# A fused landmark-attention and FFT-mixing kernel: where the landmark sums stand in VectorE's order, and a later due time for the sum of C's transposed parts

## The chip, the cores and the metric

One Trainium2 chip, one of its cores. The metric is the device time of one execution in microseconds (us). Before the change the median of three runs is 1006.84 us (1006.77 to 1008.21). A core has five engines that run side by side, each with its own instruction stream: TensorE (PE, matmuls), VectorE (DVE), ScalarE (ACT), GpSimd (POOL) and SyncE (SP), which here issues the DMAs. An engine takes its instructions in the order in which they stand in its stream; an instruction that waits for another engine holds up all that stand behind it.

## What is computed

Cut to what matters, for q, k, v of 8 batches, 8 heads, 576 positions, head size 64, and landmarks of 18 positions each (32 a head):

```python
q_lm = q.reshape(B, H, 32, 18, D).mean(axis=3)
k_lm = k.reshape(B, H, 32, 18, D).mean(axis=3)
A, Bm, C = sm(q, k_lm), sm(q_lm, k_lm), sm(q_lm, k)    # softmaxes of scaled products
Z = Bm.T / (norm1(Bm) * norminf(Bm) + 1e-6)
for _ in range(6):
    Z = 2 * Z - Z @ Bm @ Z
x = A @ Z @ C @ v                                      # heads side by side: 8 x 576 x 512
u = x + real(fft(fft(x, axis=1), axis=2))
un = (u - mean(u)) / sqrt(var(u) + 1e-6)
out = u + relu(un @ w_ch1) @ w_ch2                     # 512 -> 2048 -> 512
```

## The kernel before

The work is written as Python generators, each for one strand: `tokens(b)` (sums of landmarks, softmax A), `landmarks(b)` (products with the landmark sums, Bm, C, the six steps of Z, then the combined tables and `mix`), `values(b)` (C times v), `mix(b)` (A and the FFT tables give u; then `norm`), and `mlp()`, which takes u two tiles of 128 rows (a chunk) at a time through both weight matrices. `run()` steps the generators in a planner's time, `self.now`, and thereby writes the program down. PE's instructions keep the order in which they are written, so that attention's matmuls are strewn between those of the MLP. The other engines' instructions are put in an order by a scheduler, as far as no dependency and no added rule says otherwise.

The class `Timed` wraps DVE, ACT and POOL (V, A, G in the code). For each instruction it keeps the planned time of its result in `there` and appends its planned start to the engine's `log`. Its added rule is this: if an input is in the set `slow` (a DMA's result, or POOL's), the instruction is put behind the last one of its engine whose planned start is not after that input's planned arrival. The same can be asked for by setting `late` ahead of an instruction; `late` is back at 0 after each. Every instruction that goes through Timed is recorded under line 138, every matmul under 245, so a profile tells them apart by their tiles.

What matters here, with the names of tiles as the profile writes them:

- `load(b + 1)`, called at the end of landmarks(b), issues the DMAs of k, q and v of the next batch into tiles `big`. So k and q are in memory long before tokens(b + 1) is planned.
- In `tokens(b)`, for each half e of the heads: one sum over k (`lm<-big`, 128x64 out of 128x1152) and two over q (128x32 out of 128x576) on DVE, and one |q| with its sum on ACT (`big<-big` 128x1168, which gives `amax`). `kmax<-lm`, `qsum<-amax` and a few steps on 128x1 (`aq_e`, `aq_r`, `kb`) follow, then the splits of q into two 16-bit parts on ACT and DVE (`big<-big,aq_r`, two of 128x1024 and two of 128x128). For b = 1 the sums are kept in program order.
- `landmarks(b)` starts with PE's `at<-lm` and `at<-big,lm`; DVE makes `Bd`, `cmx`, `bmx`, `bs`, `nrm`, `BTd` of them, and PE takes up `at<-nrm,ones_bd` and `at<-BT,BTd`. Then come `RE` and `E`, and PE's six steps `at<-RE,E`.
- `values(b)` from batch 2 on: C (a tile `mid`) is cut into two 16-bit parts by ACT and POOL, these are transposed by DMA (line 588, `mid<-mid`), and DVE adds the transposed parts (`mid<-mid` 128x640). The tile of the transposed parts, th, is in `slow`, with a planned arrival 4.0 us after the parts.
- `mix(b)`: DVE makes `w<-at,scw,w` and `u<-at,scw,w`. The last 64 rows of two batches share one tile u (`uR` in the code), taken from a pool of 7, whose tiles come free when the DMA to `out_dram` has read them. `norm`: `bn`, `mv`, `ve`, `rt`, `r`, `row` on DVE and POOL, then two DMA transposes a tile to `unT`, which the MLP's first matmuls `h<-unT,w` read.
- `mlp()`: h takes two PSUM banks; ACT and DVE make `h<-h` of each. The second matmuls `acc<-w,h` gather into two PSUM banks, acc0 and acc1, of which there is one set: the next chunk's first acc matmul waits until DVE's `u<-acc,wsc,u` has read the bank. The output DMA follows each u.

Of the kernel before, what the change touches and what calls it, by code (L numbers as in the profile page):

```python
# [158 lines left out]
class Kernel:  # L159
# [82 lines left out]
    def mm(self, out, a, b, start=True, stop=True, share=1.0):  # L242
        self.there[out.name] = self.now
        self.now += share * (1.0e-3 if a.dtype == F32 else 0.42e-3) * math.prod(b.shape[1:])
        self.nc.tensor.matmul(out, a, b, start=start, stop=stop, skip_group_check=True)  # L245

    def tr(self, out, a, ident):
        self.there[out.name] = self.now
        self.now += 0.11
        self.nc.tensor.transpose(out, a, ident)  # L250
# [171 lines left out]
    def tokens(self, b, st):  # L422

        nc, mm, mm3, tr, sm, split = self.nc, self.mm, self.mm3, self.tr, self.sm, self.split
        V, A = self.V, self.A
# [5 lines left out]
        qhs = []  # L431
        for e in range(2):
            kf, qf = loads[e][0][:, 0 : 2 * S], loads[e][1][:, 0:NQ]
            first = V.tensor_reduce(lm[:, 1, e], kf.rearrange("p (m t) -> p m t", t=18), AX.X, ALU.add)
            if b == 1:
                self.tc.keep_in_program_order(first)

            lv = lm[:, 0, e].rearrange("p (x o m) -> p x o m", o=2, m=8)
            qv = qf.rearrange("p (x o t) -> p x o t", o=2, t=2 * SEG)
            for o in range(2):  # L440
                first = V.tensor_reduce(lv[:, :, o], qv[:, :, o, o : o + 144].rearrange("p x (m t) -> p x m t", t=18), AX.X, ALU.add)
                if b == 1:
                    self.tc.keep_in_program_order(first)
            qhs.append(self.big().bitcast(F16))
            A.activation((self.whole[0].bitcast(F16) if b == 0 else qhs[e])[:, 0:NQ], qf, AF.Abs, accum_out=am[:, e : e + 1])
            yield self.till(lm)
# [63 lines left out]
        for u in range(3):  # L510
# [8 lines left out]
            if b >= 2 or u == 2:  # L519
                yield self.till(ae)  # L520
                hl = self.row(2 * w, F16).rearrange("p (y t) -> p y t", y=2)
# [43 lines left out]
    def values(self, b, st, loads, Ces, crs, ci):  # L565

        nc, mm, tr, sm = self.nc, self.mm, self.tr, self.sm
        V, A = self.V, self.A
        R0 = sm.tile([P, 2, 64], F32, name="R0", bufs=1)
        ETs = []  # L570
        for g in range(2):
            yield self.till(Ces[g])
            if b < 2:
                ET = self.mid().rearrange("p (t m) -> p t m", t=5)
                ps = self.psum()
                for t in range(4):
                    tr(ps[:, 128 * t : 128 * t + 128], Ces[g][:, 128 * t : 128 * t + 128], self.ident)
                A.copy(ET[:, 0:4].rearrange("p t m -> p (t m)"), ps)
                ps = self.psum()
                tr(ps[:64, 0:128], Ces[g][:, 512:576], self.ident)  # L580
                A.copy(ET[:64, 4], ps[:64, 0:128])
            else:

                hl, th = (self.mid().bitcast(F16).rearrange("p (y t) -> p y t", y=2) for _ in range(2))
                A.copy(hl[:, 0], Ces[g])
                self.G.tensor_tensor(hl[:, 1], Ces[g], hl[:, 0], ALU.subtract)
                for y in range(2):
                    nc.sync.dma_start_transpose(th[:, y].rearrange("p (t m) -> p t m", m=P), hl[:, y])
                self.there[th.name] = self.there[hl.name] + 4.0
                self.slow.add(th.name)  # L590
                V.tensor_tensor(Ces[g], th[:, 0], th[:, 1], ALU.add)
                ET = Ces[g].rearrange("p (t m) -> p t m", t=5)
            ETs.append(ET)
        for g in range(2):
            yield self.till(ETs[g], loads[0][2], loads[1][2], banks=1)
            vfs = [loads[e][2].rearrange("p (c d) -> p c d", c=5) for e in range(2)]
            ps = self.psum()
            for t in range(5):
                n = P if t < 4 else 64
                for i in range(4):  # L600
                    e, at = divmod(sum(GROUPS, []).index(HEADS[g][i]), 4)
                    v = vfs[e][:n, t, 64 * at : 64 * at + 64]
                    mm(ps[32 * i : 32 * i + 32, 0:64], ETs[g][:n, t, 32 * i : 32 * i + 32], v if at % 2 == i % 2 else v[:, ::-1], t == 0, t == 4)
            V.tensor_scalar(R0[:, g], ps[:, 0:64], crs[g], ci[:, g : g + 1], ALU.mult, ALU.mult)
        st["R0"] = R0
# [480 lines left out]
```

## Time and profile before

| | |
|---|---|
| median of three runs | 1006.84 us (1006.77 to 1008.21) |
| the profiled execution | 1008.58 us |
| its span in the trace | 1006.8 us |
| mean granted clock of PE | 0.976 of full speed |
| PE busy | 959.8 us (95%) |
| DVE busy | 600.5 us (60%) |
| ACT busy | 333.0 us (33%) |
| POOL busy | 102.8 us (10%) |

The durations below come from the profiled execution, whose own time is 1.74 us above the median and 1.8 us above its span. A row of a timeline gives the start in us from the span's start, the duration, engine, line, operation, output and inputs, and in brackets the idle time of the engine ahead of it with what ended it; neighbouring instructions of one kind are one row with their count. A row of the waits gives who waits for whom, the sum in us, how many times, and the longest. In a table of windows, PEclk is the clock granted to PE as a share of full speed.

### The profile page before, as it was taken

The page shows a single profiled execution, that of the slowest core. Times are in us where ns is not written, and L with a number is a line of the kernel's source. Part 1 is how long each engine was busy: PE and PEld are TensorE (multiplying, and loading weights), DVE is VectorE, ACT ScalarE, POOL GpSimd, SP SyncE. Part 2 cuts the span into 40 slices and gives each one's busy share as a digit, 9 for nine tenths or more (in the row PEclk, how much of TensorE's full clock was granted, in tenths as well). Part 3 has the DMA queues.
Part 4 walks back from the last instruction along what each step waited for, and adds up shares of the span by engine and source line. Part 5 has one row for each costly group of instructions (what it writes and reads, how often), then busy time and mean ns, then how long its engine had stood idle before and what let it go on. Part 6 is the DMA issues. An engine that isn't in the chain of part 4 may idle for free.

```text
span 1006.8 us, 20849 instructions
## 1 busy us (share of the span) xinstructions
PE 959.8 (95%) x8698; PEld 666.9 (66%) x8698; DVE 600.5 (60%) x1629; ACT 333.0 (33%) x716; POOL 102.8 (10%) x114
## 2 busy tenths in 40 slices
PE   6869989699999999999999999999999999999998
PEld 4658556467766767667666677676666776666665
DVE  7989876878476836388367736684643935241111
ACT  5668543243224322143224222332322323111110
POOL 0000000003011301032012201120020210010000
PEclk8879989989999999999999999999999999999999
DMA  9854104123302340134211340225020200120000
GB/s 330 290 210 145 62 2 169 22 54 83 136 17 48 63 157 12 32 51 100 100 43 29 45 168 9 55 44 187 1 53 22 53 10 22 22 54 21 1 21 21
DMA packets 97774, 74.66 MB, mean 74 GB/s; under 512 B 68112, under 2 KB 86544, under 8 KB 97552
## 3 DMA queue, kind: packets, MB, share of 16 engines
q1 hardware_dynamic: 97680, 73.34, 25.4%
q8 instruction: 68, 1.11, 0.4%
q14 instruction: 26, 0.21, 0.1%
HBM read 48.02 MB, written 9.44 MB: 57 GB/s over the span
## 4 chain that ended last, share of the span: by engine, by line
PE 86%; DVE 9%; ACT 2%; DMA 2%; issue 1%; POOL 1%; SPq 0%; DVEq 0%; ACTq 0%; POOLq 0%
PE acc L245 36%; PE h L245 36%; PE at L245 13%; DVE w L138 2%; DVE mid L138 1%; DVE u L138 1%; DVE lm L138 1%; DMA big<-k_dram 1%; PE at L250 1%; DVE row L138 0%; ACT w L138 0%; DMA mid<-mid 0%; DMA out_dram<-u 0%; DVE asum L138 0%; DVE bn L138 0%
## 5 line engine op out<-in xcount | busy, mean ns | idle before, releaser
L245 PE MATMUL h<-unT,w 128*128 128x256 f16 x3456 | 411.4, 273 | 6.7 <-DMA unT<-row 5.4
L245 PEld LDWEIGHTS <-w 128*128 128x128 f16 (+1 forms) x3584 | 346.0, 99 | 80.9 <-DMA unT<-row 5.8
L245 PE MATMUL acc<-w,h 128*128 128x512 f16 x1632 | 386.2, 382 | 1.8 <-DVE w L138 1.8
L245 PEld LDWEIGHTS <-h 128*128 128x128 f16 x1632 | 157.8, 99 | 166.6 <-issue 14.2
L138 DVE SCALAR_TENSOR_TENSOR h<-h 128x512 f16<-128x512 f32 x136 | 93.6, 688 | 207.1 <-ACT h L138 206.7
L138 ACT ACTIVATE h<-h 128x512 f16<-128x512 f32 x136 | 81.0, 596 | 319.2 <-PE h L245 313.1
L138 POOL TENSOR_TENSOR r<-ve,mhalf 128x2 f32<-128x2 f32 (+1 forms) x20 | 13.8, 689 | 495.7 <-DVE ve L138 477.0
L138 DVE TENSOR_REDUCE lm<-big 128x32 f32<-128x576 f32 (+1 forms) x48 | 44.4, 938 | 3.3 <-DMA big<-k_dram 3.1
L245 PEld LDWEIGHTS <-big 128*128 128x128 f16 (+1 forms) x864 | 40.5, 104 | 8.5 <-issue 2.1
L138 DVE TENSOR_TENSOR mid<-mid 128x256 f32<-128x256 f32 (+3 forms) x64 | 38.4, 633 | 7.9 <-DMA mid<-mid 6.4
L138 POOL TENSOR_TENSOR mid<-mid 128x640 f16<-128x640 f32 (+1 forms) x24 | 30.6, 1292 | 117.0 <-ACT mid L138 102.5
L245 PEld LDWEIGHTS <-mid 64*128 64x128 f16 (+1 forms) x624 | 29.2, 95 | 17.1 <-issue 10.8
L138 POOL TENSOR_TENSOR row<-row 128x512 f16<-128x512 f32 (+1 forms) x33 | 34.1, 1048 | 50.1 <-ACT row L138 50.1
L138 DVE SCALAR_TENSOR_TENSOR u<-at,scw,w 128x128 f32<-128x128 f32 (+3 forms) x105 | 33.7, 388 | 7.2 <-PE at L245 5.5
L138 ACT CAST row<-row 128x512 f16<-128x512 f32 (+1 forms) x40 | 20.8, 551 | 51.6 <-DVE row L138 44.6
L138 DVE SCALAR_TENSOR_TENSOR w<-at,scw,w 128x262 f32<-128x262 f32 (+1 forms) x42 | 19.1, 486 | 29.7 <-ACT w L138 29.6
L138 DVE SCALAR_TENSOR_TENSOR u<-acc,wsc,u 128x512 f32<-128x512 f32 x36 | 26.9, 749 | 11.8 <-PE acc L245 11.7
L245 PE MATMUL at<-mid,big 128*128 128x262 f16 (+1 forms) x288 | 33.2, 289 | 0.0
L245 PEld LDWEIGHTS at<-RE,E 128*128 128x128 f32 x192 | 26.8, 194 | 8.4 <-issue 2.8
L245 PE MATMUL at<-RE,E 128*128 128x64 f32 (+1 forms) x192 | 28.8, 273 | 3.2 <-DVE E L138 2.5
L138 DVE SCALAR_TENSOR_TENSOR big<-big,aq_r 128x1024 f16<-128x1024 f32 (+1 forms) x32 | 25.8, 840 | 3.5 <-ACT big L138 3.5
L138 DVE TENSOR_TENSOR E<-at,mask 128x256 f32<-128x256 f32 x40 | 16.7, 418 | 18.3 <-PE at L245 18.3
(178 smaller groups left out, 916.8 us busy)
## 6 DMA issues: line engine op xcount, KB each, us to landing
w<-w_dram SPq DMA_DIRECT2D x22, 512.0 KB, 7.0
big<-v_dram SPq DMA_DIRECT2D x16, 640.0 KB, 9.5
big<-q_dram SPq DMA_DIRECT2D x16, 584.0 KB, 6.1
big<-k_dram SPq DMA_DIRECT2D x16, 576.0 KB, 5.2
out_dram<-u SPq DMA_DIRECT2D x36, 256.0 KB, 2.0
big<-w_dram SPq DMA_DIRECT2D x10, 512.0 KB, 6.6
t<-t_dram SPq DMA_DIRECT2D x1, 1048.0 KB, 10.6
unT<-row SPq DMA_TRANSPOSE x64, 2.4
```

The lines of the kernel that those rows point to most:

```text
L138: ins = call(out, *args, **kw)
L245: self.nc.tensor.matmul(out, a, b, start=start, stop=stop, skip_group_check=True)
L250: self.nc.tensor.transpose(out, a, ident)
```

## The change

In `tokens`, ahead of the sum over k, `late` of DVE and ACT is set to the planner's present time; ahead of each of the two sums over q, that of DVE is. So each sum, and ACT's sum of magnitudes, is put behind the last instruction of its engine whose planned start is not after that time. In `values`, the planned arrival of the transposed parts of C is set 2.5 us later. The whole diff:

```diff
@@ -431,6 +431,7 @@
         for e in range(2):
             kf, qf = loads[e][0][:, 0 : 2 * S], loads[e][1][:, 0:NQ]
+            V.late = A.late = self.now
             first = V.tensor_reduce(lm[:, 1, e], kf.rearrange("p (m t) -> p m t", t=18), AX.X, ALU.add)
@@ -438,6 +439,7 @@
             for o in range(2):
+                V.late = self.now
                 first = V.tensor_reduce(lv[:, :, o], qv[:, :, o, o : o + 144].rearrange("p x (m t) -> p x m t", t=18), AX.X, ALU.add)
@@ -586,7 +588,7 @@
-                self.there[th.name] = self.there[hl.name] + 4.0
+                self.there[th.name] = self.there[hl.name] + 6.5
                 self.slow.add(th.name)
                 V.tensor_tensor(Ces[g], th[:, 0], th[:, 1], ALU.add)
```

The engines' instructions are the same in number and kind; their order differs. In batch 0 nothing moves, in batch 1 only ACT's first |q|, which goes behind three more splits of weights. From batch 2 on, the sums move on DVE.

The first place is DVE in the mix of batch 1, around the norm of its first two tiles (`w_74` is a part of the second weight buffer that serves as scratch, `r_2574` and `r_2576` are small tiles of the norm). Before:

```order
L138 BN_STATS bn<-u 128x6 x2
L138 BN_AGGR mv<-bn 128x2
L138 TENSOR_REDUCE lm<-big 128x4x8
L138 BN_AGGR mv<-bn 128x2
L138 SCALAR_TENSOR_TENSOR h<-h 128x512
L138 TENSOR_SCALAR ve<-mv 128x2
L138 TENSOR_REDUCE lm<-big 128x4x8
L138 TENSOR_TENSOR rt<-r_2574 128x2
L138 TENSOR_REDUCE lm<-big 128x64
L138 SCALAR_TENSOR_TENSOR rt<-rt,ve 128x2
L138 TENSOR_REDUCE kmax<-lm 128x1
L138 SCALAR_TENSOR_TENSOR r_2576<-rt,r_2574 128x2
```

And after the change, at the same place:

```order
L138 BN_STATS bn<-u 128x6 x2
L138 BN_AGGR mv<-bn 128x2 x2
L138 TENSOR_SCALAR ve<-mv 128x2
L138 SCALAR_TENSOR_TENSOR h<-h 128x512
L138 TENSOR_TENSOR rt<-r_2574 128x2
L138 SCALAR_TENSOR_TENSOR rt<-rt,ve 128x2
L138 SCALAR_TENSOR_TENSOR r_2576<-rt,r_2574 128x2
L138 TENSOR_SCALAR row<-u,mv,r_2576 128x512 x2
L138 TENSOR_TENSOR row<-row 128x512 x2
```

The sums of batch 2 and its kmax are gone from here, and the norm's steps follow one another.

The second place is DVE ahead of the landmarks of batch 2, where they now stand (`acc_2163` and `acc_2164` are acc0 and acc1 of the chunk that ends, `r_2780` and `r_2782` small tiles of the norm of the last rows). Before:

```order
L138 TENSOR_TENSOR rt<-r_2780 128x1
L138 TENSOR_TENSOR kb<-kmax,aq_e 128x1
L138 SCALAR_TENSOR_TENSOR rt<-rt,ve 128x1
L138 SCALAR_TENSOR_TENSOR r_2782<-rt,r_2780 128x1
L138 TENSOR_SCALAR row<-u,mv,r_2782 128x512
L138 SCALAR_TENSOR_TENSOR big<-big,aq_r 128x1024
L138 SCALAR_TENSOR_TENSOR h<-h 128x512
L138 TENSOR_TENSOR row<-row 128x512
L138 SCALAR_TENSOR_TENSOR u<-acc_2163,wsc,u 128x512
L138 SCALAR_TENSOR_TENSOR u<-acc_2164,wsc,u 128x512
L138 SCALAR_TENSOR_TENSOR big<-big,aq_r 128x128
L138 SCALAR_TENSOR_TENSOR big<-big,aq_r 128x1024
```

And after the change:

```order
L138 TENSOR_REDUCE lm<-big 128x64
L138 SCALAR_TENSOR_TENSOR r_2782<-rt,r_2780 128x1
L138 TENSOR_REDUCE lm<-big 128x4x8
L138 TENSOR_SCALAR row<-u,mv,r_2782 128x512
L138 TENSOR_REDUCE lm<-big 128x4x8
L138 SCALAR_TENSOR_TENSOR u<-acc_2163,wsc,u 128x512
L138 TENSOR_TENSOR row<-row 128x512
L138 SCALAR_TENSOR_TENSOR u<-acc_2164,wsc,u 128x512
L138 SCALAR_TENSOR_TENSOR h<-h 128x512
L138 TENSOR_REDUCE kmax<-lm 128x1
L138 TENSOR_TENSOR qsum<-amax 128x1
L138 TENSOR_SCALAR aq_e<-qsum 128x1
```

Three of the six sums stand just ahead of the first u<-acc here, the other three a little before; the splits of q, which stood on both sides of u<-acc, now follow behind `Bd`.

The third place is DVE in the mix of batch 5, around its last 64 rows, ahead of the landmarks of batch 6. Before, the sums of batch 6 stood further ahead, among the steps for the first four tiles:

```order
L138 TENSOR_SCALAR row<-u,mv,r_8389 128x512 x2
L138 SCALAR_TENSOR_TENSOR h<-h 128x512
L138 SCALAR_TENSOR_TENSOR w_74<-at,scw,w_73 64x262 x2
L138 SCALAR_TENSOR_TENSOR u<-at,scw,w_74 64x256
L138 SCALAR_TENSOR_TENSOR u<-at,scw,w_74 64x128 x2
L138 TENSOR_TENSOR qsum<-amax 128x1
L138 BN_STATS bn<-u 128x6
L138 TENSOR_SCALAR aq_e<-qsum 128x1
L138 BN_AGGR mv<-bn 128x2
```

And after the change:

```order
L138 TENSOR_SCALAR row<-u,mv,r_8389 128x512 x2
L138 SCALAR_TENSOR_TENSOR h<-h 128x512
L138 TENSOR_REDUCE lm<-big 128x64
L138 SCALAR_TENSOR_TENSOR w_74<-at,scw,w_73 64x262 x2
L138 SCALAR_TENSOR_TENSOR u<-at,scw,w_74 64x256
L138 SCALAR_TENSOR_TENSOR u<-at,scw,w_74 64x128 x2
L138 TENSOR_REDUCE lm<-big 128x4x8
L138 BN_STATS bn<-u 128x6
L138 TENSOR_REDUCE lm<-big 128x4x8
L138 BN_AGGR mv<-bn 128x2
```

The first three sums now stand among these steps, the other three and kmax some rows further on, still ahead of `qsum`.

## Prediction

> **What bounds the kernel now.** I read the page's span, engine and chain lines first.
>
> ```profile
> span 1006.8 us, 20849 instructions
> ...
> PE 959.8 (95%) x8698; PEld 666.9 (66%) x8698; DVE 600.5 (60%) x1629; ACT 333.0 (33%) x716; POOL 102.8 (10%) x114
> ...
> PE 86%; DVE 9%; ACT 2%; DMA 2%; issue 1%; POOL 1%; SPq 0%; DVEq 0%; ACTq 0%; POOLq 0%
> ```
>
> TensorE (PE) is busy for 95%, and the change takes no matmul away, so the time can only move where PE stands still. VectorE (DVE), 60% busy, is the engine whose order changes. Next, the waits of PE, summed over the span; these rows, and a wait of 2.4 for w that the timeline below shows, are those that the change can shorten.
>
> ```profile
> PE h L245 <- DMA unT<-row: 5.4, 2, 3.2
> ...
> PE at L245 <- DVE E L138: 2.5, 1, 2.5
> ...
> PE at L245 <- DVE u L138: 1.6, 2, 0.8
> ```
>
> In total 5.4 + 2.4 + 2.5 + 1.6 = 11.9 us can be won; where DVE gets later at any other place, time can only be lost. The waits for unT and w lie in the mix of batch 1, shown here in PE's timeline.
>
> ```profile
> 194.92 0.49 PE L245 MATMUL at<-Wx,mid 64*128 64x128 f16 x11 [2.37 <-DVE w L138]
> 198.59 0.40 PE L245 MATMUL h<-unT,w 128*128 128x256 f16 x1 [3.18 <-DMA unT<-row]
> 201.18 1.04 PE L245 MATMUL h<-unT,w 128*128 128x256 f16 x4 [2.19 <-DMA unT<-row]
> ```
>
> **What is moved.** The page's groups of the sums, of the splits of q that follow them on DVE, and of a step of ScalarE:
>
> ```profile
> L138 ACT ACTIVATE h<-h 128x512 f16<-128x512 f32 x136 | 81.0, 596 | 319.2 <-PE h L245 313.1
> ...
> L138 DVE TENSOR_REDUCE lm<-big 128x32 f32<-128x576 f32 (+1 forms) x48 | 44.4, 938 | 3.3 <-DMA big<-k_dram 3.1
> ...
> L138 DVE SCALAR_TENSOR_TENSOR big<-big,aq_r 128x1024 f16<-128x1024 f32 (+1 forms) x32 | 25.8, 840 | 3.5 <-ACT big L138 3.5
> ```
>
> 44.4 us in 8 batches is 5.6 us for each batch's six sums; the four splits of a batch, two long (1.3) and two short (0.3), are 25.8 / 8 = 3.2. They now stand where k and q have just arrived, in gaps of DVE. By the order that results, held against the times at which DVE's neighbouring rows ran, they come some 14 to 46 us later, just ahead of the chain of landmarks(), which PE needs soon after. No DMA moves on SP and nothing is added on POOL. So the sum has one gain and six places where 5.6 us are pushed into a denser stretch.
>
> **Batch 1's mix, the gain.** DVE's timeline there:
>
> ```profile
> 184.66 1.34 DVE L138 TENSOR_REDUCE lm<-big 128x64 f32<-128x1152 f32 x1
> ...
> 189.01 0.72 DVE L138 TENSOR_REDUCE lm<-big 128x32 f32<-128x576 f32 x1
> ...
> 190.38 0.74 DVE L138 TENSOR_REDUCE lm<-big 128x32 f32<-128x576 f32 x1
> ...
> 191.34 0.16 DVE L138 TENSOR_TENSOR rt<-r 128x2 f32<-128x2 f32 x1 [0.22 <-POOL r L138]
> 191.42 1.34 DVE L138 TENSOR_REDUCE lm<-big 128x64 f32<-128x1152 f32 x1
> ...
> 192.80 0.29 DVE L138 TENSOR_REDUCE kmax<-lm 128x1 f32<-128x128 f32 x1
> ...
> 193.47 0.99 DVE L138 TENSOR_SCALAR row<-u,mv,r 128x512 f32<-128x512 f32 x2
> ```
>
> 1.34 + 0.72 + 0.74 + 1.34 + 0.29 = 4.43 us of sums for batch 2 stand ahead of the row that the transposes to unT wait for. Without them the POOL step that now costs 0.22 shows more of itself, so not all is won: I take the rows 3.4 us earlier. PE's three waits there, 2.37 + 3.18 + 2.19 = 7.74, end 3.4 us earlier: **-3.4**. At the start, ScalarE's first sum of magnitudes of batch 1 moves behind three weight splits, which so run sooner, and PE waits for them there: **-0.4**, an estimate between 0 and 0.6, one step of ScalarE.
>
> **Batch 2's landmarks, the first place that pays.** DVE, then PE:
>
> ```profile
> 217.10 1.40 DVE L138 SCALAR_TENSOR_TENSOR u<-acc,wsc,u 128x512 f32<-128x512 f32 x2
> ...
> 223.89 0.18 DVE L138 TENSOR_TENSOR nrm<-diag,rs 128x64 f32<-128x64 f32 x1
> ...
> 218.19 1.46 PE L245 MATMUL acc<-w,h 128*128 128x512 f16 x6
> ...
> 226.02 0.38 PE L245 MATMUL at<-nrm,ones_bd 128*128 128x128 f32 x2
> ```
>
> u<-acc frees the two PSUM banks that the next chunk's acc matmuls need; the first of the two ends at 217.8, 0.4 us ahead of them. Ahead of it now come 5.6 us of sums, while a split of 1.3 us and the small steps around it (1.2) go behind it and 1.4 us of idle time (waits for ScalarE and POOL shortly before) are used up: it is 1.7 us later, so PE waits 1.3 for the first bank and, since one 0.7 us step now stands between the two u<-acc, 0.5 more for the second. Then nrm: it had 226.02 - 224.07 = 1.95 us to spare, but the split work of 3.3 us that was ahead of it now lies inside its chain: it is late by a further 1.2. Together **+3.0**.
>
> **The mixes of batches 2 and 6, with the sums of batches 3 and 7 in them: two like places.** DVE and PE in the first, then the page's row of the output DMA; the second shows the same wait of 0.8, as the row on u above counts it twice.
>
> ```profile
> 317.57 0.75 DVE L138 SCALAR_TENSOR_TENSOR u<-acc,wsc,u 128x512 f32<-128x512 f32 x1
> ...
> 320.45 0.99 DVE L138 SCALAR_TENSOR_TENSOR u<-at,scw,w 64x256 f32<-64x256 f32 x3 [0.83 <-DMA out_dram<-u]
> ...
> 320.98 1.23 PE L245 MATMUL at<-big,lm 64*32 64x288 f32 x16 [0.79 <-DVE u L138]
> ...
> out_dram<-u SPq DMA_DIRECT2D x36, 256.0 KB, 2.0
> ```
>
> A chain is there already: u<-acc, its output DMA (2.0), then the u that takes the freed buffer, whose reading of PSUM frees banks for PE. Three sums and kmax (3.0 us) now come between h and the splits that precede u<-acc; 1.5 us of splits move behind it. u<-acc comes 1.5 us later, and the chain has no slack, since PE waits for it now: **+1.5** each, **+3.0**.
>
> **The landmarks of batches 4 and 6.** DVE's nrm against PE's use of it, and the idle time of DVE in batch 6 that could take the sums in:
>
> ```profile
> 446.26 0.18 DVE L138 TENSOR_TENSOR nrm<-diag,rs 128x64 f32<-128x64 f32 x1
> ...
> 448.67 0.38 PE L245 MATMUL at<-nrm,ones_bd 128*128 128x128 f32 x2
> ...
> 643.79 0.91 DVE L138 SCALAR_TENSOR_TENSOR w<-at,scw,w 64x262 f32<-64x262 f32 x2 [0.70 <-ACT w L138]
> ...
> 647.50 0.16 DVE L138 TENSOR_TENSOR rt<-r 128x1 f32<-128x1 f32 x1 [0.54 <-POOL r L138]
> ...
> 652.68 0.69 DVE L138 SCALAR_TENSOR_TENSOR h<-h 128x512 f16<-128x512 f32 x1 [0.41 <-ACT h L138]
> ...
> 654.76 0.29 DVE L138 TENSOR_SCALAR Bd<-at 128x32 f32<-128x32 f32 x2 [1.39 <-PE at L245]
> ...
> 657.92 0.18 DVE L138 TENSOR_TENSOR nrm<-diag,rs 128x64 f32<-128x64 f32 x1
> ...
> 660.33 0.39 PE L245 MATMUL at<-nrm,ones_bd 128*128 128x128 f32 x2
> ```
>
> In batch 6, DVE's idle time adds up to 0.70 + 0.54 + 0.41 + 1.39 = 3.0 us. Of 5.9 us (sums and kmax), 2.9 stay; the first split then waits about 1 us for ScalarE, whose sum of magnitudes has moved later too, and one split of 0.3 comes into the chain: nrm is 4.0 to 4.2 later against a slack of 660.33 - 658.10 = 2.2: **+1.8**. In batch 4 the slack is 448.67 - 446.44 = 2.2 as well; two splits (1.6) enter the chain and Bd is 3 later: **+2.3**.
>
> **Batch 5, and the sum of C's parts.** DVE, PE, and the windows table (its clock stands third from the end):
>
> ```profile
> 559.57 0.82 DVE L138 TENSOR_TENSOR mid<-mid 128x640 f32<-128x640 f16 x1 [2.23 <-DMA mid<-mid]
> ...
> 551.64 2.75 PE L245 MATMUL acc<-w,h 128*128 128x512 f16 x12
> ...
> 560.87 0.63 PE L245 MATMUL at<-RE,E 128*128 128x64 f32 x4 [2.46 <-DVE E L138]
> ...
> 561.93 4.45 PE L245 MATMUL acc<-w,h 128*128 128x512 f16 x12
> ...
> 562.00:565.40 3.40, 3.40 (x9) 1.21 (x10) 3.40 (x9) 1.47 (x3) 0.00 (x0) 0.50 0.00 0
> ```
>
> Here E stands behind the second sum of C's parts, which waits for its transposes. The raise from 4.0 to 6.5 should put that sum behind E; in the order that results only the first sum moves, past one reciprocal, and the second still precedes E. So I cost this edit at nothing, between -4.2 (the wait of 2.46 and what follows it, below) and +2.5 (the whole raise shows on the path). What counts is that the landmarks before it are later by the sums: transposes, sum and E come 1.7 later, with no slack: **+1.7**.
>
> After that wait of 2.46, the granted clock is 0.50 for one window of 3.4 us, and twelve matmuls take 4.45 in place of 2.75: such a window costs 1.7. The wait of 0.79 in batch 2's mix is not followed by one. The new or grown waits, of 1.2 to 2.3, lie between these two; I count one window for all of them together, **+1.7**, with none and three (5.1) as ends. The Trainium skill ("TensorE: Matmul & The Clock Gate", section "HAM oscillation — how this bites in real kernels") names gaps of more than some 3.4 us as what throttles TensorE. The row of 2.46 speaks against reading that as a safe limit. By that rule this term would be nothing.
>
> **The sum.** -3.4 - 0.4 + 3.0 + 3.0 + 1.8 + 2.3 + 1.7 = +8.0, with the clock +9.7. The profiled execution took 1008.58 (span 1006.8), so it becomes 1018.3. It lies 1.74 above the median of the three runs before, 1006.84, which gives 1016.5.
>
> **Rivals.**
>
> 1. Faster: the queue absorbs the sums. The 14 to 46 us by which they move hold idle DVE time, 40% of the span, and three of my six places have a slack of about 2 us, so that a backlog that is 2 us shorter than I have it costs nothing there. If the sums slip into such gaps and the backlog has drained by the time that u<-acc, Bd and E are reached, only batch 1's gain is left: -3.8, 1003.0; and with one window of half clock less behind its shorter waits, 1001.3. It decides where less than 2.2 us of the 5.9 are left at Bd and none at u<-acc. For it: DVE is idle for 3.0 us just there in batch 6. Against it: 5.9 us are to fit in these 3.0. Chance 0.20.
> 2. No change: a third of the 11.8 comes, about +4, against -3.8: 1007. It would be so if about two of the six places pay, and the others, each a lateness of 1.2 to 2.3 after about 2 us of slack, come out within it. Against it: three of them (both mixes and batch 5) have no slack at all. Chance 0.12.
> 3. The raised 6.5 frees E in batch 5, -4.2: the sum is +5.5 or less, 1012.3. Against it stands the order. Chance 0.10.
> 4. No new stall trips the clock: all of them are shorter than the 2.46 that did. +8.0, 1014.8. Chance 0.18. The rule of the Trainium skill told above, by its page's figure, gives this case.
> 5. My forecast, 1016.5, with one window, more where two or three trip (up to 1020): 0.40.
>
> A change of 0.2%, 2.0 us, is about what a measurement of this kernel can tell from none. Faster takes rival 1, 0.20; the same takes rival 2, 0.12; slower is the rest, 0.68. The likeliest sign's own range is 1011 to 1020. The range takes in all the slower cases up to three windows and reaches down to rival 1's 1003, so that what it leaves out is the lower part of rival 1 and what lies above 1020, together under 0.2: 1002.5 to 1020.
>
> **What would show it.** In the changed kernel PE's waits for unT in batch 1's mix should sum to about 4.4 in place of 7.7; PE should wait for u ahead of the first acc matmul of a chunk in batch 2 and for nrm in batches 2, 4 and 6 by 1 to 2.5 us each, rows that are not there now; the two waits for u in the mixes should be 2.3 in place of 0.8; the wait for E in batch 5 should grow, or be gone (rival 3). If PE shows no wait for nrm, the forecast's sign is wrong. If batch 1's waits stay at 7.7, the gain was not there, and the time is 3.4 higher.

## Result and profile after

The changed kernel takes 1020.37 us (median of 4 runs, 1017.26 to 1022.66), the kernel before beside it 1007.4 us (4 runs, 1006.77 to 1008.21): ratio 1.0126, 95% interval 1.0098 to 1.0155. It is slower, as forecast; the time lies 0.4 us above the upper end of the range and 3.9 above the forecast. The profiled execution took 1017.26 us, the shortest of the four. Its page:

```profile
span 1015.3 us, 20860 instructions
...
PE 961.4 (95%) x8698; PEld 666.9 (66%) x8698; DVE 603.5 (59%) x1629; ACT 331.3 (33%) x716; POOL 100.4 (10%) x114
...
PE 72%; DVE 15%; issue 6%; ACT 3%; POOL 2%; DMA 1%; SPq 0%; DVEq 0%; POOLq 0%; ACTq 0%
```

The work is the same; the span is 8.5 us longer, and in the chain that ended last PE's share falls from 86% to 72% and DVE's rises from 9% to 15%. PE's waits, the rows that moved:

```profile
PE at L245 <- ACT mid L138: 11.3, 5, 4.0
PE at L245 <- DVE u L138: 5.1, 2, 2.6
...
PE h L245 <- DMA unT<-row: 3.6, 2, 2.3
...
PE acc L245 <- DVE u L138: 2.9, 2, 1.5
...
PE at L245 <- DVE E L138: 2.3, 1, 2.3
...
PE at L245 <- DVE w L138: 0.9, 1, 0.9
...
PE at L245 <- DVE nrm L138: 0.4, 1, 0.4
```

Two of these rows before the change, which the prediction doesn't show:

```profile
PE at L245 <- ACT mid L138: 6.2, 2, 4.0
...
PE acc L245 <- DVE u L138: 1.4, 1, 1.4
```

The waits for unT and w fell from 7.7 in all to 4.5; those for u in the mixes rose from 1.6 to 5.1, those for u ahead of acc from 1.4 to 2.9, and those for `mid` of ScalarE from 6.2 to 11.3. The last was not in the prediction's list. Where each lies, in PE's timeline: batch 1's mix and batch 2.

```profile
193.65 0.49 PE L245 MATMUL at<-Wx,mid 64*128 64x128 f16 x11 [0.90 <-DVE w L138]
195.38 0.28 PE L245 MATMUL h<-unT,w 128*128 128x256 f16 x1 [1.25 <-DMA unT<-row]
197.97 3.30 PE L245 MATMUL h<-unT,w 128*128 128x256 f16 x17 [2.31 <-DMA unT<-row]
...
215.22 1.02 PE L245 MATMUL acc<-w,h 128*128 128x512 f16 x4 [1.52 <-DVE u L138]
```

Behind batch 1's shorter waits there is less half clock as well. The windows table gives a stretch, its length, the busy time of PE (then of the other engines), and third from the end the granted clock. Before, the clock was 0.50 for three windows, from 196.8 on; the last two of them, and then the one in the same place after the change, where only the window from 197.2 to 200.6 was at half clock:

```profile
200.20:203.60 3.40, 2.42 (x12) 1.75 (x13) 1.88 (x7) 0.00 (x0) 0.69 (x1) 0.50 0.11 22
203.60:207.00 3.40, 3.40 (x31) 2.18 (x29) 0.00 (x0) 0.47 (x1) 0.00 (x0) 0.50 0.00 0
```

```profile
200.61:204.02 3.41, 3.41 (x41) 2.32 (x40) 1.31 (x3) 1.84 (x4) 0.00 (x0) 1.00 0.00 0
```

And the later places, each with its wait (the mix of batch 2, the landmarks of batches 4, 5 and 6, the wait for E in batch 5, the mix of batch 6):

```profile
321.09 1.23 PE L245 MATMUL at<-big,lm 64*32 64x288 f32 x16 [2.55 <-DVE u L138]
...
449.36 0.16 PE L245 MATMUL at<-kb,ones 128*128 128x1 bf16 x1 [1.65 <-ACT mid L138]
...
451.00 0.46 PE L245 MATMUL at<-nrm,ones_bd 128*128 128x128 f32 x2 [0.16 <-ACT RE L138]
...
553.53 0.16 PE L245 MATMUL at<-kb,ones 128*128 128x1 bf16 x1 [0.91 <-ACT mid L138]
...
564.53 0.63 PE L245 MATMUL at<-RE,E 128*128 128x64 f32 x4 [2.30 <-DVE E L138]
...
665.12 0.16 PE L245 MATMUL at<-kb,ones 128*128 128x1 bf16 x1 [2.10 <-ACT mid L138]
...
789.13 1.23 PE L245 MATMUL at<-big,lm 64*32 64x288 f32 x16 [2.55 <-DVE u L138]
```

The same matmuls read against the rows of before give PE's lag at each place: -3.2 at the last wait for unT (201.18, now 197.97), +0.1 at the mix of batch 2 (320.98, now 321.09), +2.3 at batch 4's nrm (448.67, now 451.00), +3.7 at E (560.87, now 564.53), and +8.5 at the end. So the gain came, was given back by the mix of batch 2, and the rest of the batches added the loss.

In batches 4 to 6 the new wait stands at the small matmul on kb, and its releaser is not kb. Batch 4, DVE's timeline first:

```profile
439.67 2.66 DVE L138 TENSOR_REDUCE lm<-big 128x64 f32<-128x1152 f32 x3
...
443.08 0.14 DVE L138 TENSOR_TENSOR kb<-kmax,aq_e 128x1 bf16<-128x1 f32 x1
444.45 1.28 DVE L138 SCALAR_TENSOR_TENSOR big<-big,aq_r 128x1024 f16<-128x1024 f32 x1 [1.23 <-ACT big L138]
...
446.26 0.28 DVE L138 TENSOR_SCALAR Bd<-at 128x32 f32<-128x32 f32 x2
...
449.13 1.28 DVE L138 SCALAR_TENSOR_TENSOR big<-big,aq_r 128x1024 f16<-128x1024 f32 x1
...
450.67 0.19 DVE L138 TENSOR_TENSOR nrm<-diag,rs 128x64 f32<-128x64 f32 x1
```

Then ScalarE's:

```profile
448.72 0.50 ACT L138 ACTIVATE mid<-at,cb 128x288 f32<-128x288 f32 x1 [0.90 <-DVE cb L138]
```

kb itself was ready at 443.2. But its matmul needs a free PSUM bank. Attention's products share four banks in the kernel, and the four tiles of landmark products fill them until ScalarE's exp of C (`mid<-at,cb`) has read the first; that exp waits for cb, which stands in DVE's late chain. The exp ends at 449.2, and PE goes on at 449.36. Bd is 3.2 us later than before (443.10), nrm 4.4 later (446.26); since PE has already stood 1.65 at kb, only 0.16 is left to wait ahead of nrm.

### The profile page after: what moved, and what is told of

Same layout as the page of the kernel before. It is cut to its first block, busy times and chain, and to the rows that moved or that the text cites. A ratio compares the mean times of both kernels' runs of the same rounds, so it can differ in the third digit from the quotient of the medians.

```text
span 1015.3 us, 20860 instructions
## 1 busy us (share of the span) xinstructions
PE 961.4 (95%) x8698; PEld 666.9 (66%) x8698; DVE 603.5 (59%) x1629; ACT 331.3 (33%) x716; POOL 100.4 (10%) x114
## 4 chain that ended last, share of the span: by engine, by line
PE 72%; DVE 15%; issue 6%; ACT 3%; POOL 2%; DMA 1%; SPq 0%; DVEq 0%; POOLq 0%; ACTq 0%
PE h L245 30%; PE acc L245 30%; PE at L245 12%; DVE w L138 3%; DVE lm L138 2%; DVE u L138 2%; DVE mid L138 2%; DVE big L138 1%; DVE row L138 1%; DVE h L138 1%; POOL row L138 1%; ACT big L138 1%; DVE cmx L138 1%; DMA big<-k_dram 1%; DVE asum L138 1%
## 5 line engine op out<-in xcount | busy, mean ns | idle before, releaser
L138 ACT ACTIVATE big<-big,aq_r 128x1024 f16<-128x1024 f32 (+1 forms) x32 | 23.0, 774 | 17.5 <-DVE kb L138 15.7
```

The lines of the kernel that those rows point to most:

```text
L138: ins = call(out, *args, **kw)
```

## Experiments

Theory: DVE's queue ahead of u<-acc and of the landmarks' chain, lengthened by 5.6 us of sums in each batch from 3 on, makes the loss; batch 2 is even; the due time does nothing; how many of the new waits are followed by a window of half clock sets the rest. Rivals: the later due time has a part, or the late values of the sums, or ScalarE's delayed sums of magnitudes.

**Parts of the change.** Four kernels: the late lines alone, the due time alone, late for batch 2 alone, and for batches 3 to 7 alone (the last two with the due time at 4.0):

```diff
-            V.late = A.late = self.now
+            if b >= 3:            # or: if b == 2
+                V.late = A.late = self.now
...
-                V.late = self.now
+                if b >= 3:
+                    V.late = self.now
```

> The three late lines alone, the due time of C's parts left at 4.0. My theory: the landmark sums make the whole difference and the due time none, so the time is that of the full change, 1.009 to 1.015 times that of before (1016 to 1022 us), with PE's waits for u in the mixes of batches 2 and 6 at about 2.5 us each. Rival (the later due time carries a good part of the loss): 1.004 to 1.007, below 1014 us. Rival (it hides a gain): above 1023 us.

> The due time 6.5 alone, the sums as before. My theory: it moves nothing that PE waits for, ratio 0.998 to 1.002 (1005 to 1009 us), and batch 5's wait for E stays at about 2.4 us. Rival (it costs): 1.003 or more. Rival (it frees E in batch 5): 0.996, 1003 us, with no wait for E.

> late is set for batch 2's sums alone, due time 4.0. My theory: the gain in batch 1's mix (3.4 us of waits, and up to 1.7 per window of half clock that goes with them) against 2.7 us at batch 2's landmarks: -0.7 to -3, ratio 0.997 to 0.999 (1004 to 1007 us). Rival (the gain in batch 1's mix isn't one of these sums): ratio 1.002 or more, since only the cost is left.

> late is set from batch 3 on alone, due time 4.0. My theory: 1.8 + 2.5 + 1.1 + 2.7 + 1.85, about 10 us of PE's waits in batches 3 to 7, without batch 1's gain: 1017 to 1023 us, ratio 1.010 to 1.016, thus as slow as the full change or slower. Rival (the loss lies in batch 2): ratio below 1.005.

| kernel | median us | ratio to before (95%) |
|---|---|---|
| late lines alone | 1023.45 | 1.0136 (1.0114 to 1.0158) |
| due time alone | 1008.93 | 0.9998 (0.9986 to 1.0010) |
| late for batch 2 alone | 1008.75 | 1.0002 (0.9989 to 1.0015) |
| late for batches 3 to 7 alone | 1023.58 | 1.0152 (1.0136 to 1.0169) |

The loss is that of batches 3 to 7. The late lines alone lie in their forecast by the ratio; their 1023.45 us is just above the 1023 that the second rival named, but the interval of the ratio overlaps that of the full change, so no gain of the due time is shown. The due time alone changes nothing in the time, as costed, and batch 5's wait for E is still there (2.0 in its profile). It does change the order, by more than the prediction says: in its trace 1265 of PE's 8698 matmuls stand elsewhere in PE's order than before (compared by tiles and shapes), since the planner waits 2.5 us longer with the products of C. Batch 2 alone is even, which neither my forecast (0.997 to 0.999) nor the rival (1.002) had: what batch 1's mix gains is paid back.

**What in the sums costs.** First, the same from batch 3 on with `V.late` but without `A.late`.

> As the run with late from batch 3 on, but ScalarE's sums of magnitudes are left where they were before. My theory: the loss is DVE's queue ahead of Bd and u<-acc; ScalarE's share is at most the wait of 1.2 us for the first split in batches 4 and 6, so the ratio is 1.011 to 1.015. Rival (ScalarE's delayed sum of magnitudes, through qsum, makes the loss): below 1.006.

It took 1022.02 us, 1.0126 (1.0104 to 1.0147). That is 0.26% less than with ScalarE's sums moved too, and the intervals overlap, so a share of ScalarE's isn't shown; the larger part of the loss is there without it.

Then the kernel before, its real sums where they were, and six more for a tile lmx that nothing reads, from batch 3 on, bound by `late` as the change binds the real ones (names, arguments and some of the planner's bookkeeping cut):

```diff
+            if b >= 3:
+                V.late = self.now
+                V.tensor_reduce(self.lmx[:, 1, e], kf..., AX.X, ALU.add)
+                for o in range(2):
+                    V.late = self.now
+                    V.tensor_reduce(lx[:, :, o], qx..., AX.X, ALU.add)
             first = V.tensor_reduce(lm[:, 1, e], ...)
```

> All real sums and magnitudes stay where they were before; from batch 3 on, six sums more of the same shapes, which nothing reads, are put where the change puts the real ones (output unchanged). My theory: what PE pays is the 5.6 us of DVE time ahead of the landmarks' chain, not the late arrival of the sums: ratio 1.008 to 1.015, with new waits of PE for u in the mixes of about 2 us and at the matmul on kb in batches 4 and 6. Rival (the late values of the sums or of kmax make the loss): below 1.003.

It took 1019.96 us, 1.0119 (1.0100 to 1.0137). PE's waits in it:

```profile
PE at L245 <- ACT mid L138: 11.0, 5, 4.0
...
PE at L245 <- DVE u L138: 3.9, 2, 2.0
```

Here lm and kmax are as early as before, and the same two rows grow (6.2 to 11.0 and 1.6 to 3.9). So DVE's time ahead of these places is enough for most of the loss, without any lateness of what the sums yield; whether that lateness has a part in the rest (1.0119 here, 1.0126 and 1.0152 with the real sums moved) is not shown. Two things differ from the change: DVE has 5.6 us a batch more to do in all, and not every extra sum lands where the real ones do. In the mix of batch 2 the second three start at 316.49, behind kb (313.38) and the first split of q; in the changed kernel the second three stand ahead of kmax, kb and that split. The next kernel doubles the dose: twelve in place of six.

> As the run with six sums more that nothing reads, but twelve of them (11 us) at the same places, from batch 3 on (output unchanged). My theory: the slack of about 2 us at each place is used up by the first six, so the second six cost their whole 5.6 us in each of five batches, less what of PE's waits DVE can use: 15 to 28 us more, ratio 1.027 to 1.040. Rival (the loss comes from the order, the time of the sums hardly matters): ratio below 1.017.

It took 1026.67 us, 1.0175 (1.0150 to 1.0200): by the ratios 5.6 us above the dose of six, not 15 to 28, and just above the rival's bound of 1.017, which lies inside the interval. My step from one dose to two was wrong. DVE ahead of the mix of batch 2's last u, with six and with twelve:

```profile
316.49 2.66 DVE L138 TENSOR_REDUCE lmx<-big 128x64 f32<-128x1152 f32 x3
319.07 1.54 DVE L138 SCALAR_TENSOR_TENSOR big<-big,aq_r 128x128 f16<-128x128 f32 x2
...
321.13 0.74 DVE L138 SCALAR_TENSOR_TENSOR u<-acc,wsc,u 128x512 f32<-128x512 f32 x1
```

```profile
304.37 3.92 DVE L138 TENSOR_REDUCE lmx<-big 128x64 f32<-128x1152 f32 x4
...
311.36 5.24 DVE L138 TENSOR_REDUCE lmx<-big 128x64 f32<-128x1152 f32 x6
...
317.11 0.74 DVE L138 SCALAR_TENSOR_TENSOR u<-acc,wsc,u 128x512 f32<-128x512 f32 x1
...
319.15 1.55 DVE L138 SCALAR_TENSOR_TENSOR big<-big,aq_r 128x1024 f16<-128x1024 f32 x2 [0.51 <-ACT big L138]
```

With six, u<-acc (321.13) stands behind splits and sums; with twelve, the scheduler has put the splits behind u<-acc (317.11), and between 304.37 and the split at 319.15 DVE has no idle time left. More work in one place changes the order around it, so doubling a load is no clean measure where a scheduler sets the order.

**Batch 2's gain.** Is it lost only because the sums go just ahead of u<-acc? This kernel binds batch 2's sums to the `row` steps of batch 1's first norm (`V.late = self.mark`) instead of the planner's time; three then land there, three ahead of u<-acc.

> Batch 2's sums alone are moved, but put behind the first row of the first norm in batch 1's mix in place of the planner's present time: three land there and three just ahead of u<-acc. My theory: batch 1's waits lose their 3.4 us as in the change, and the wait for u ahead of the chunk's first acc matmul falls to under 1 us: -2 to -4 against before, ratio 0.996 to 0.998 (1004 to 1007 us). Rival (what is gained at a wait in the mix of batch 1 is lost again wherever the sums go): 0.9995 or more.

It took 1008.86 us, 1.0008 (0.9994 to 1.0021): no gain. PE's waits in it are

```profile
195.04 0.49 PE L245 MATMUL at<-Wx,mid 64*128 64x128 f16 x11 [1.84 <-DVE w L138]
195.84 0.28 PE L245 MATMUL h<-unT,w 128*128 128x256 f16 x1 [0.31 <-DMA unT<-row]
198.43 3.81 PE L245 MATMUL h<-unT,w 128*128 128x256 f16 x17 [2.31 <-DMA unT<-row]
...
223.20 0.16 PE L245 MATMUL at<-kb,ones 128*128 128x1 bf16 x1 [1.35 <-ACT mid L138]
...
226.15 0.46 PE L245 MATMUL at<-nrm,ones_bd 128*128 128x128 f32 x2 [1.47 <-ACT RE L138]
```

The first three add up to 4.46, 3.3 us less than before; 2.8 come back at kb and nrm, where before had no wait. A further kernel also gives those matmuls more time: late for batch 2, its landmark products and kb planned HOLD (2.5) later, and batch 5's second sum behind E (below).

> late for batch 2's sums alone, batch 2's landmark products and the matmul on kb planned 2.5 us later on PE, and batch 5's second sum behind E. Theory (batch 1's gain of 3.4 us is lost at batch 2's landmarks only because PE comes to them too early): the waits of 1.7 and 1.0 there go, and with E's 3 to 4 the ratio is 0.992 to 0.995 (1000 to 1004 us). Rival (DVE itself is full from the mix of batch 1 to batch 2's softmax, so the wait comes elsewhere in batch 2): 0.996 to 0.998, E's gain alone.

It took 1004.53 us, 0.9962 (0.9947 to 0.9977), which is E's part alone: the rival's range, not my 0.992 to 0.995. These three kernels show no net gain from batch 2. Why the gain is always paid back stays open. The rival's reason, that DVE is full from batch 1's mix to batch 2's softmax, is not what the trace of the run before this one shows, where DVE stands idle in one piece ahead of the last tiles of batch 1's mix:

```profile
204.14 0.50 DVE L138 SCALAR_TENSOR_TENSOR w<-at,scw,w 64x262 f32<-64x262 f32 x1 [4.63 <-ACT w L138]
```

In all three kernels some or all of batch 2's sums stand behind this wait, in none do they all stand ahead of it; no run put the later three, 2.8 us, into the 4.63.

**The sum of C's parts and E.** The kernel before with the one exchange that a later due time could have brought, in batch 5 alone:

```diff
-                V.tensor_tensor(Ces[g], th[:, 0], th[:, 1], ALU.add)
+                both = V.tensor_tensor(Ces[g], th[:, 0], th[:, 1], ALU.add)
+                if b == 5 and g == 1:
+                    self.tc.add_manual_dep(both.ins, st["E"], info, reason="behind E")
```

(Cut: a loop that holds values(5) back in the planner until E is written, and the line that notes E's name.) In the trace, these two instructions of DVE are the only ones that stand elsewhere than before.

> The kernel before with two neighbouring instructions of DVE exchanged in batch 5: the second sum of C's parts stands behind E, which a later due time might have done. Theory (that wait of DVE for a DMA holds up E): PE's wait for E, 2.46, and its window of half clock go, -2.5 to -4.2, ratio 0.996 to 0.9975. Rival (the time comes back at the next matmul that waits, on R0 or Yd): ratio 0.999 or more.

It took 1005.03 us, 0.9969 (0.9954 to 0.9985): 0.3% faster than before. DVE and then PE there:

```profile
556.88 0.43 DVE L138 TENSOR_TENSOR E<-RE,mask 128x256 f32<-128x256 f32 x1
559.13 0.82 DVE L138 TENSOR_TENSOR mid<-mid 128x640 f32<-128x640 f16 x1 [1.82 <-DMA mid<-mid]
```

```profile
557.76 0.64 PE L245 MATMUL at<-RE,E 128*128 128x64 f32 x4
...
558.82 2.76 PE L245 MATMUL acc<-w,h 128*128 128x512 f16 x12
```

DVE still waits 1.82 for the DMA, but E is done by then, PE does not wait at all, and the twelve matmuls take 2.76 in place of 4.45. Of the rival, 0.54 us comes back as a wait for RE at 572.12. The same exchange in the changed kernel:

> The changed kernel with the second sum of C's parts put behind E in batch 5. Theory (that wait is a separate matter from the sums): PE's wait for E of 2.3 us goes, with its window of half clock, -2.3 to -4 against the changed kernel, so ratio 1.007 to 1.010 to before. Rival (since the sums make DVE late there, the wait moves to another instruction): the ratio of the changed kernel, 1.011 or more.

It took 1016.89 us, 1.0082 (1.0065 to 1.0099): 0.4 to 0.5% below the changed kernel. Within the intervals the two matters add up.

**The clock.** The changed kernel again:

> The changed kernel once more, unaltered, beside the others of this call, for the spread of its runs and the mean granted clock of each. My theory (the new waits of 1.5 to 2.6 us trip a window of half clock in some executions and not in others): runs from 1017 to 1023 us, the longer ones with the lower mean clock, ratio 1.010 to 1.015. Rival (a fixed loss with random noise): runs within 3 us of each other and no order by clock.

It took 1021.99 us (4 runs, 1020.13 to 1023.11), 1.0130 (1.0110 to 1.0149). The runs stand in order of their mean granted clock: 1020.13 and 1021.42 at 0.978, 1022.56 and 1023.11 at 0.973. They also lie within 3 us of each other, as the rival had it, so these four alone decide little; the traces decide. In this kernel's profiled execution three of the new waits (mix of batch 2, landmarks of batch 6, mix of batch 6) are followed by a window of half clock. Here are the three, by windows that start and end about where the clock may change (PE's busy time stands after the length, the clock third from the end), and then the first place in the first profile of the changed kernel:

```profile
317.07:320.49 3.42, 1.16 (x16) 0.31 (x16) 3.42 (x12) 0.04 (x1) 0.00 (x0) 1.00 0.41 153
320.49:323.90 3.41, 3.41 (x24) 2.41 (x18) 2.99 (x19) 2.22 (x9) 0.00 (x0) 0.50 0.03 5
...
661.80:665.24 3.44, 1.40 (x10) 0.81 (x9) 3.44 (x16) 0.86 (x4) 0.00 (x0) 1.00 0.00 0
665.24:668.65 3.41, 3.37 (x12) 1.90 (x11) 3.03 (x22) 3.41 (x11) 0.65 (x1) 0.50 0.01 2
...
788.10:791.50 3.40, 1.12 (x16) 0.31 (x16) 3.40 (x12) 0.00 (x1) 0.00 (x0) 1.00 0.41 154
791.53:794.94 3.41, 3.41 (x24) 2.41 (x18) 2.97 (x19) 2.24 (x9) 0.00 (x0) 0.50 0.02 5
```

```profile
316.67:320.08 3.41, 1.87 (x41) 0.84 (x39) 3.41 (x7) 0.86 (x2) 0.00 (x0) 1.00 0.37 139
320.08:323.50 3.42, 2.41 (x28) 1.44 (x29) 3.42 (x18) 0.26 (x1) 0.00 (x0) 1.00 0.06 20
```

The wait in the mix is 2.55 us in both. In the one it falls into a single window, PE is busy for 1.16 of it, and the next window is at half clock. In the other it is split over two, with 1.87 and 2.41 busy, and the clock stays. PE's busy time alone does not draw a sharp line between the two: a window with 1.61 busy was followed by half clock in the changed kernel with E's exchange (784.14 to 787.55) and not in the first profile of the changed kernel (661.41 to 664.82), and one with 1.82 was in the kernel without `A.late` (563.34 to 566.75). The Trainium skill ("TensorE: Matmul & The Clock Gate", section "What's actually happening") says that the activity window is 3413 ns long and runs free of the kernel; the rows agree, with 3.41 us and a phase that differs between executions. The rule of the Trainium skill ("TensorE: Matmul & The Clock Gate", section "HAM oscillation — how this bites in real kernels"), that gaps over some 3.4 us throttle, does not hold as a limit here: 2.55 is enough when it falls right.

## Why the prediction came out as it did

- **The gain in batch 1's mix (-3.4)**: right, 7.74 to 4.46, -3.3. The start's -0.4 was not to be seen: the first h matmul came 0.2 later. The opening varies by more than that: ahead of batch 1's mix, at 192 us, the second profile is 2.5 us ahead of before, and that of the extra six sums, whose opening is the same as before's, 2.4 behind.
- **Batch 2 (+3.0)**: PE's lag rises by 3.3 between the rows at 201.18 and 320.98; the mix's 1.75 is in it, and 1.4 of half clock saved behind batch 1's shorter waits, which the sum left at nothing (the lag falls to -4.65 at the h matmuls at 210.36, now 205.71), so batch 2 itself cost 3.0. The wait for u ahead of acc is 1.52 for the 1.8 worked out; nrm's is 0.35 and not 1.2, the rest lies in smaller waits.
- **The mixes of batches 2 and 6 (+1.5 each)**: right, 2.55 in place of 0.8, +1.75 each.
- **Batches 4 and 6 (+2.3, +1.8)**: the chain is right. Bd was to be 3 us later and is 3.2 in batch 4; PE's lag there grew by 2.2. In batch 6 it grew by 2.3 up to nrm (660.33, now 666.44), the wait at kb alone is 2.1, and by 0.6 more before the batch's mix. The instruction was wrong: PE stops at kb for a PSUM bank, ahead of nrm. I had followed the data and not the bank. So the sign that I named, no wait for nrm, would have misled: those waits are 0.35 in batch 2, 0.16 in batch 4 and none in batch 6, and the change is slower all the same.
- **Batch 5 (+1.7)**: it paid at kb, 0.91; the wait for E was 2.30, no longer than before, since PE had come as late to it as the transposes. PE's lag grew by 1.3 from batch 4's nrm to E.
- **The due time (0)**: right, 0.9998.
- **The clock (+1.7, ends 0 and 5.1)**: the step that failed, by its size. I counted one window of half clock for all new waits together. The second profile shows three behind new waits, and over them PE's lag against before grows by 1.65, 1.63 and 1.65 beyond the waits: 4.9 us where the sum has 1.7. The other profiles with the sums of batches 3 to 7 moved show two or three (late lines alone three; batches 3 to 7 alone, without `A.late`, and with E's exchange two each). The first profile, with none, is the exception.
- **The sum of the waits (+8.0)**: low as well, by 1 to 2 us. In the first profile PE's lag grows from +0.2 ahead of batch 1's mix to +8.5 at the end, with 1.4 of saved half clock in it: 9.7. In the second it grows from -2.5 to +11.4, of which 4.9 is half clock: 9.0. The largest parts are the landmarks of batch 6 (some 2.8 for 1.8), the two mixes (3.5 for 3.0) and the start (0 for -0.4).

Together: against the kernel before that ran beside it the changed kernel lost 13.0 us, where 9.7 was forecast. My upper end, three windows on top of 8.0, is 13.1; it was passed because that kernel before was 0.6 us slower than the 1006.84 from which the range was counted. That the profiled execution (1017.26) lies only 1.0 below the 1018.3 that I had for it is luck: its waits are 1.7 above my sum, its clock 3.1 below my term.

Rival 1, that the queue absorbs the sums, is out by the run from batch 3 on; rival 3's mechanism exists (-4.2 forecast, and the exchange gave 0.9969, 3 us), but as the order showed, the change doesn't bring it about. Rival 4, no window at all, fits the first profile (1017.26 where it has 1016.6 as a profiled execution) and none of the others.

## What to carry to other kernels

Work that is off the critical path may stand in the idle time of its engine or just ahead of a chain that another engine waits for; the total doesn't change, the time does, so look for the slack at the new place and not at the old one. Follow PSUM banks as well as data when a chain gets late: the first matmul to stop may be one whose inputs have long been there. Where a wait stands ahead of a matmul-bound stretch, price it with the clock window that it may trip, and give the count a range.

## What the runs showed of the hardware

A stall of PE can cost more than its length: 1.6 to 1.7 us more for each window of 3.41 us that follows at half clock in a stretch full of matmuls. The same stall of 2.55 us trips it in one execution and not in another, according to how it lies to the windows (PE busy for 1.40 us or less of a window tripped it, 1.87 did not, 1.61 went both ways). Much of the spread between runs of one kernel goes with the mean granted clock of the run: of 21 runs of the kernel before, the seven at 0.979 or more took 1006.2 to 1007.4 us, the three at 0.974 or less 1010.6 to 1011.8.
